# A gated MLP behind attention: the last rows' side work cut into small pieces, its operands by VectorE, and the order of the low parts

## Chip, cores and metric

One core of one Trainium2 chip. The metric is the device time of one execution in microseconds (us), as the median of a few runs. PE is TensorE's matmul stream (PEld its weight loads), DVE is VectorE, ACT is ScalarE, POOL is GpSimd, SP is SyncE, whose queue issues most DMAs.

## The reference

```python
mod = (silu(c) @ w_mod).reshape(1, 6, 1, 576)     # sa, ca, ga, sb, cb, gb
h = layernorm(x) * (1 + ca) + sa                  # x: 1 x 2048 x 576
x = x + ga * attention(h, wqkv, wo)               # 32 heads of 18
h = layernorm(x) * (1 + cb) + sb
x = x + gb * ((sigmoid(h @ w_gate) * (h @ w_up)) @ w_down)   # F = 4608
```

Everything is float32. The kernel splits each float32 operand of a product into a high part (a cast to `fp32r`) and a low part (the difference), and sums high x high, high x low and low x high.

## The kernel before

The program has two stages. The first, up to 1602 us, is projections and attention. In its last part it also makes the second layer norm of rows 0 to 1023 and writes their operands to DRAM; of rows 1024 to 2047 it has only done most of the output projection (`x1p`, and `oend` for the columns that come last). The second stage is the gated MLP, and the change lies wholly in it.

**Turns.** `seq` is a list of 252 turns: 2 halves of the rows, 18 blocks of 256 MLP columns (`NB`), 7 products each, in the order `ORDER` = 1, 6, 2, 7, 5, 4, 3; turn 6 is below the turn of product 6, and so on. Seven products replace eight, since a block of 2 x 2 products (gate and up over two groups of 128 columns, two groups of 512 rows) is formed by a scheme of Strassen's kind. One product is 14 matmuls of 128x128 by 128x512 (`product`, L1050). Their left operands `w` come from the raw weights or from sums of them (`S1`, `S2`, `S3`, made on POOL by `weights_sums`); the right operands `X` are seven operands of the rows, which stay in SBUF for a whole half.

**Weights.** In the first half of the turns the weights are made while the turns run, `LOOK` = 4 turns ahead: `weights_high` copies the high part on ACT (L1031), `weights_low` subtracts the low part on DVE (L1040, L1041) and saves the operand to DRAM over SP (`ws`, L1042). The table `LOWS` says in which turn which low part is made; the three of turn 7 stand one after the other, behind the turn's down sums. In the second half the weights come back by DMA.

**A block.** Product 1 is copied by ACT to `p1`. DVE adds products and partial sums (L1254, L1265, L1270, L1276, L1281). Products 2, 5, 4 and 3 complete one gated group each: `gate` takes the sigmoid (ACT), the product with the other half (DVE), the high part `hh` (ACT); `gate_low` the low part `hl` (DVE, L1070), in the same turn. In turns 6 and 7 of the *next* block PE makes the down sums (`down`, L1090): 8 sums per turn, 6 matmuls of 128x288 each, into a PSUM pool `pd` of 3 buffers; DVE adds each sum into `Oa` (L1094), and this frees the buffer.

**The last rows.** While the first half's turns run, the operands of rows 1024 to 2047 must be made for the second half. The generator `last_rows` does it in steps: the end of the output projection (PE, DVE), layer norm statistics and scaling (DVE, some POOL), transposes (PE) that ACT scales and SP writes to DRAM (`ln_spill`, `hs`), and at last, three times, `operand_parts`: from four 128x512 blocks the seven operands, with high parts by ACT (L729) and the differences and low parts by POOL (L731, L736, L740), written to `xs`. The main loop takes steps of it from block 0's turn 5 on, in turns 6 and 7 of each block, and in others where a step has been marked as light by yielding `True`. In the last block of the first half, `X` is reloaded from `xs`, one operand per turn.

**Order.** From turn 7 on (`ORDERED`) the order of PE, DVE and ACT is that of the program's text; POOL and SP follow a scheduler. Each engine works in order: an instruction that waits holds all behind it.

Of the kernel before, what the change touches and what calls it, by code (L numbers as in the profile page):

```python
# [15 lines left out]
F32 = mybir.dt.float32  # L16
# [27 lines left out]
LOOK = 4  # L44
LOWS = ((2,), (2,), (2,), (2, 3, 4), (), (3,), ())
NB = F // 256
# [6 lines left out]
ORDERED = 7  # L53
ROWS_FROM = 4
SECOND = 7 * NB
# [3 lines left out]
def tile_block(ctx, tc, x_in, wqkv, wo, w_gate, w_up, w_down, c_in, w_mod, out):  # L59
# [646 lines left out]
    def ln_spill(zs, ch, psum, pool, put):  # L706


        for g in range(2):
            for i in range(3):  # L710
                pt = psum()
                for j, z in enumerate(zs):
                    nc.tensor.transpose(pt[:, j * P : (j + 1) * P], z[:, g, i * P : (i + 1) * P], ident)
                ev = pool.tile([P, 512], F32, name="ev", bufs=2)
# [339 lines left out]

    def gate(st, t, f, r):

        if t is None:
            t = ep.tile([P, 512], F32, name="sg")
            nc.scalar.activation(t, st["a"][0], AF.Sigmoid)  # L1059
            nc.vector.tensor_mul(t, st["a"][1], t)  # L1060
        else:
            nc.scalar.activation(t[:, 0:512], t[:, 0:512], AF.Sigmoid)  # L1062
            nc.vector.tensor_mul(t[:, 0:512], t[:, 0:512], t[:, 512:1024])  # L1063
            t = t[:, 0:512]
        nc.scalar.copy(st["hh", r][:, f, :], t)  # L1065
        return st, t, f, r
# [9 lines left out]

    def down(st, r):

        wh, wl = st["wd"]
        hh, hl = st["hh", r], st["hl", r]  # L1080
        for j in range(4):
            t = 4 * r + j
            rows = slice(j * P, (j + 1) * P)
            for h in range(2):
                cols = slice(h * HALF, (h + 1) * HALF)
                acc = pd.tile([P, 512], F32, name="d")
                n = 0
                for f in range(2):
                    for a, w in ((hh, wh), (hh, wl), (hl, wh)):
                        nc.tensor.matmul(  # L1090
                            acc[:, :HALF], a[:, f, rows], w[:, f, cols], start=n == 0, stop=n == 5
                        )
                        n += 1
                nc.vector.tensor_add(Oa[:, t, cols], Oa[:, t, cols], acc[:, :HALF])  # L1094
# [35 lines left out]
    pd = ctx.enter_context(tc.tile_pool(name="pd", bufs=3, space=PSUM))  # L1130

    def last_rows():


        def psum():
            return pd.tile([P, 512], F32, name="d")

        with tc.tile_pool(name="fin", bufs=1, side="right") as pool:
            w = pool.tile([P, 2, 2, D], F32R, name="w")
            nc.gpsimd.dma_start(w, wod)  # L1140
            for t0 in (0, 4):
                od = pool.tile([P, 4, 256], F32, name="od")
                nc.sync.dma_start(od[:, :, 0:192], oend[:, t0 : t0 + 4, :])
                nc.sync.dma_start(od[:, :, 192:256], oend[:, t0 : t0 + 4, 128:192])
                yield True
                yield
                pt = psum()
# [5 lines left out]
                nc.vector.tensor_sub(ol, pt, oh.bitcast(F32))  # L1153
                yield
                pt = psum()
# [4 lines left out]
                nc.vector.tensor_copy(om[0:64], pt[0:64])  # L1160
                nc.vector.tensor_copy(omh[64:P], pt[64:P])
                nc.vector.tensor_sub(om[64:P], pt[64:P], omh[64:P].bitcast(F32))
                xts = []
                for j in range(-1, 4):
                    if j < 3:
                        xts.append(pool.tile([P, D], F32, name="xt", bufs=2))
                        nc.sync.dma_start(xts[-1], x1p[:, t0 + j + 1, :])
                    if j < 0:
                        yield 0
                        continue  # L1170
                    rows = slice(j * P, (j + 1) * P)
                    xt = xts[j]
                    for h in range(2):
                        cols = slice(h * HALF, (h + 1) * HALF)
                        acc = psum()
                        ts_ = ((oh, 0, 0), (oh, 1, 0), (ol, 0, 0), (om, 0, 1), (om, 1, 1))
                        for n, (a, i, k) in enumerate(ts_):
                            nc.tensor.matmul(
                                acc[:, :HALF], a[:, rows], w[:, i, k, cols], start=n == 0, stop=n == 4
                            )  # L1180
                        nc.vector.tensor_add(xt[:, cols], xt[:, cols], acc[:, :HALF])
                    nc.sync.dma_start(x1d[:, t0 + j, :], xt)
                    yield

# [3 lines left out]
        with tc.tile_pool(name="zp2", bufs=1, side="right") as zp:  # L1188
            for ch in (2, 3):
                zs = []  # L1190
                for t in range(4 * ch, 4 * ch + 4):
# [3 lines left out]
                    zs.append(z)  # L1195
                yield True
                yield
                for j, z in enumerate(zs):
                    ln_stats(zp, z[:, :, 0:HALF], mv2[:, 4 * ch + j, :])
                    if j % 2:  # L1200
                        yield
                four = slice(4 * ch, 4 * ch + 4)
                yield from ln_scales_steps(zp, mv2[:, four, :], rs2[:, four])
                for j, z in enumerate(zs):
                    ln_rows(z, 4 * ch + j, z[:, :, 0:HALF], nc.vector)
                    if j % 2:
                        yield True if j > 1 else None
                yield True
                yield from ln_spill(zs, ch, psum, zp, modulated)
        with tc.tile_pool(name="xop2", bufs=2) as pool:  # L1210
# [7 lines left out]
            for i in range(3):  # L1218
                blocks = get()
                for (g, r), t in zip(((0, 0), (0, 1), (1, 0), (1, 1)), blocks):  # L1220
                    cols = slice(HW + r * 512, HW + (r + 1) * 512)
                    nc.sync.dma_start(t, hs[g, i, :, cols])
                yield True
                yield True
                for _ in operand_parts(1, i, blocks, parts, nc.scalar.copy, nc.gpsimd, nc.sync):
                    yield True

# [6 lines left out]
    rows2 = last_rows()  # L1234
    light = True
    before = None
    for n, (hf, b, k) in enumerate(seq):
        if n == ORDERED:
            manual.enter_context(tc.manual_schedule(engines={mybir.EngineType.PE, mybir.EngineType.DVE, mybir.EngineType.Activation}))
        st, kept = block(n), None  # L1240
        if SECOND <= n + LOOK < len(seq):
            weights_high(block(n + LOOK), seq[n + LOOK][2])
        if k == 1:
# [3 lines left out]
            for v in range(2):  # L1247
                nc.scalar.copy(half(st["p1"], v), st["a"][v])
        elif k == 6:
            st["b_"] = banks()  # L1250
# [4 lines left out]
        elif k == 2:  # L1255
            product(st, 2, st["a"], False)
            for r in range(2):
                st["hh", r] = ep.tile([P, 2, 512], F32R, name=f"hh{r}")
                st["hl", r] = ep.tile([P, 2, 512], F32R, name=f"hl{r}")
            kept = gate(st, None, 0, 0)  # L1260
        elif k == 7:
# [4 lines left out]
        elif k == 5:  # L1266
            st["c"] = banks()
            product(st, 5, st["c"], True)
            for v in range(2):
                nc.vector.tensor_add(half(st["u3"], v), st["c"][v], half(st["u3"], v))  # L1270
            kept = gate(st, st["u3"], 1, 1)
            down_weights(st)
        elif k == 4:
            product(st, 4, st["b_"], False)
            for v in range(2):
                nc.vector.tensor_add(half(st["p1"], v), st["b_"][v], half(st["p1"], v))  # L1276
            kept = gate(st, st["p1"], 1, 0)
        else:
            product(st, 3, st["c"], False)
            for v in range(2):  # L1280
                nc.vector.tensor_add(half(st["u2"], v), st["c"][v], half(st["u2"], v))  # L1281
            kept = gate(st, st["u2"], 0, 1)
        if before is not None and k in (6, 7):
            down(before, k - 6)
        if n + LOOK < SECOND:
            weights_high(block(n + LOOK), seq[n + LOOK][2])
        at = n % 7
        lows = list(LOWS[at])
        if lows:
            weights_low(n + lows.pop(0))  # L1290
        if kept:
            gate_low(*kept)
        if n >= ROWS_FROM and (at in (1, 3) or light):
            light = next(rows2, None)
        while lows:
            weights_low(n + lows.pop(0))
        if n >= ROWS_FROM and (at == 1 and light is None or at in (1, 3) and light is True):
            light = next(rows2, None)
# [5 lines left out]
        if hf == 0 and b == NB - 1:  # L1304
            s = ORDER.index(k)
            nc.gpsimd.dma_start(X[s], xs[1, s])
    for r in range(2):
        down(before, r)
    manual.close()
# [27 lines left out]
```

## Time and profile before

| | |
|---|---|
| median of 3 runs | 2940.77 us (2938.65 to 2940.89) |
| the profiled execution | 2941.94 us, of it span 2940.2 us |
| PE, DVE, ACT, POOL busy | 2851.2, 2205.7, 1564.5, 707.2 us |
| first half's turns | 1602.20 to 2286.93 us, 684.73 us, PE busy 651.19, DVE busy 532.27 |
| one block of the second half | 34.96 us, PE busy 34.96 |

Rows of the profile name line, engine, operation, `out<-in` and shape; "idle before" is the time in which the engine waited ahead of the instruction, with what ended the wait. The windows view gives the busy time of each engine in a stretch, the TensorE clock that was granted (PEclk, 1.00 is full) and the DMA engines' share.

### The profile page before, as it was taken

How to read it: one execution, taken by the hardware profiler on the slowest of the kernel's cores; microseconds unless marked ns; L12 is line 12 of the kernel's file. 1: busy time of each engine (PE TensorE's matmuls, PEld its weight loads, DVE VectorE, ACT ScalarE, POOL GpSimd, SP SyncE). 2: the span in 40 equal slices, each digit the busy share in tenths (PEclk: the TensorE clock that was granted, in tenths of full speed). 3: DMA queues.
4: the chain of work that ended last, by engine and by line, in shares of the span. 5: the costliest groups of instructions: out<-in, count | busy, mean ns of one | idle time of the engine just before them, and what ended most of it. 6: DMA issues, size and time to landing. Idle time of an engine off the chain costs nothing. (4 is left out here: it accounts for less than half of the span.)

```text
span 2940.2 us, 46375 instructions
## 1 busy us (share of the span) xinstructions
PE 2851.2 (97%) x17141; PEld 1884.8 (64%) x17141; DVE 2205.7 (75%) x4015; ACT 1564.5 (53%) x2941; POOL 707.2 (24%) x869
## 2 busy tenths in 40 slices
PE   7999999999999999999999999999989999999998
PEld 5964333343444443444444888888778888888887
DVE  7277888888899988999982777878777555555555
ACT  2216889999987778998788333233332111111111
POOL 3022015444212111761103222222562100000000
PEclk9999999999999999999999999999999999999999
DMA  5344124333222110322135756565767854454443
GB/s 164 125 152 140 48 79 139 133 121 123 83 56 76 35 56 23 103 95 66 55 100 184 250 209 238 195 229 207 276 225 252 320 172 167 168 168 165 158 166 119
DMA packets 136386, 429.26 MB, mean 146 GB/s; under 512 B 19100, under 2 KB 55968, under 8 KB 123872
## 3 DMA queue, kind: packets, MB, share of 16 engines
q1 hardware_dynamic: 119664, 344.20, 34.6%
q0 software_dynamic: 16496, 82.10, 8.0%
q8 instruction: 135, 2.21, 0.3%
q14 instruction: 91, 0.75, 0.1%
HBM read 267.77 MB, written 157.95 MB: 145 GB/s over the span
## 5 line engine op out<-in xcount | busy, mean ns | idle before, releaser
L455 DVE TENSOR_REDUCE mx<-s 128x1 f32<-128x512 f32 x1696 | 1076.1, 683 | 124.2 <-PE s L449 108.0
L931 ACT ACTIVATE p<-s 128x512 f32<-128x512 f32 x2048 | 1069.1, 612 | 148.7 <-PE s L449 78.2
L449 PE MATMUL s<-k,q 54*128 54x512 f32 x1920 | 608.1, 451 | 12.8 <-ACT p L931 5.7
L551 PE MATMUL o<-p,vaug 128*32 128x512 f32 x4096 | 554.9, 607 | 0.4 <-ACT p L931 0.4
L927 PE MATMUL s<-q,k 56*128 56x512 f32 x1920 | 551.9, 425 | 0.9 <-issue 0.2
L1090 PE MATMUL d<-wd,hh 128*128 128x288 f32 x2304 | 467.7, 298 | 24.2 <-DVE Oa L1094 19.5
L927 PEld LDWEIGHTS s<-q,k 56*128 56x128 f32 x1920 | 260.4, 186 | 295.1 <-DVE mx L455 185.5
L449 PEld LDWEIGHTS s<-k,q 54*128 54x128 f32 x1920 | 273.6, 184 | 250.0 <-ACT p L931 170.9
L1090 PEld LDWEIGHTS d<-wd,hh 128*128 128x128 f32 x2304 | 377.5, 190 | 34.1 <-DVE Oa L1094 23.4
L1094 DVE TENSOR_TENSOR Oa<-Oa,d 128x288 f32<-128x288 f32 x576 | 257.7, 453 | 173.7 <-PE d L1090 169.7
L1050 PE MATMUL x<-k,w 128*128 128x512 f32 x1512 | 357.9, 391 | 2.4 <-ACT w L1031 2.4
L1090 PE MATMUL d<-wd,hl 128*128 128x288 f32 x1152 | 342.6, 297 | 0.0
L1050 PEld LDWEIGHTS x<-k,w 128*128 128x128 f32 x1512 | 282.6, 189 | 59.8 <-ACT w L1031 2.6
L1062 ACT ACTIVATE u<-u 128x512 f32<-128x512 f32 x72 | 45.5, 632 | 424.6 <-DVE u L1270 384.9
L1050 PE MATMUL x<-big,w 128*128 128x512 f32 x1008 | 238.8, 392 | 10.6 <-DVE u L1270 10.6
L1050 PE MATMUL x<-w,w 128*128 128x512 f32 x1008 | 235.2, 390 | 1.1 <-DMA w<-ws 1.1
L1050 PEld LDWEIGHTS x<-big,w 128*128 128x128 f32 x1008 | 189.2, 189 | 53.0 <-issue 12.5
L1090 PEld LDWEIGHTS d<-wd,hl 128*128 128x128 f32 x1152 | 218.7, 190 | 0.0
L1050 PEld LDWEIGHTS x<-w,w 128*128 128x128 f32 x1008 | 187.3, 188 | 38.5 <-issue 1.3
L551 PEld LDWEIGHTS o<-p,vaug 128*32 128x32 f32 x4096 | 83.4, 108 | 163.9 <-issue 152.2
L1059 ACT ACTIVATE sg<-x 128x512 f32<-128x512 f32 x36 | 21.5, 598 | 311.8 <-PE x L1050 311.7
L1096 POOL DMA_DIRECT2D out_dram<-Oa x16 | 8.7, 542 | 606.7 <-DVE Oa L1094 606.7
(215 smaller groups left out, 2996.9 us busy)
## 6 DMA issues: line engine op xcount, KB each, us to landing
ws<-w SPq DMA_DIRECT2D x126, 640.0 KB
w<-ws SPq DMA_DIRECT2D x126, 640.0 KB
wd<-wds SPq DMA_DIRECT2D x36, 1152.0 KB
k<-kd SPq DMA_DIRECT2D x60, 360.0 KB
wds<-w POOLq DMA_DIRECT2D x18, 1152.0 KB, 4.5
k<-kd SPq DMA_DIRECT2D x60, 180.0 KB
w<-in_B_w_down_dram POOLq DMA_DIRECT2D x18, 576.0 KB, 4.5
q<-qd SPq DMA_DIRECT2D x64, 144.0 KB
```

What stands on the lines that cost most here:

```text
L449: nc.tensor.matmul(sp, qs[rows, qt * P : (qt + 1) * P], ks[rows, at * 512 : (at + 1) * 512], start=True, stop=True,)
L455: nc.vector.tensor_reduce(to, sp, axis=AX.X, op=ALU.max)
L551: nc.tensor.matmul(acc[32 * j : 32 * j + 32, :], vaug[:, kt, (2 * p + h) * VW : (2 * p + h) * VW + 32], probs[2 * c + h], start=kt == 0, s ...
L927: nc.tensor.matmul(sT, ks[rows, kcols], qs[rows, c * 512 : (c + 1) * 512], start=True, stop=True)
L931: state["exp"] = nc.scalar.activation(pr, sT, AF.Exp, scale=SCALE)
L1050: nc.tensor.matmul(acc[v], w[:, v, a, :], X[s][:, b, :], start=first and n == 0, stop=n == 6, skip_group_check=not first,)
L1059: nc.scalar.activation(t, st["a"][0], AF.Sigmoid)
L1062: nc.scalar.activation(t[:, 0:512], t[:, 0:512], AF.Sigmoid)
L1090: nc.tensor.matmul(acc[:, :HALF], a[:, f, rows], w[:, f, cols], start=n == 0, stop=n == 5)
L1094: nc.vector.tensor_add(Oa[:, t, cols], Oa[:, t, cols], acc[:, :HALF])
L1096: nc.gpsimd.dma_start(out_rows[:, 8 * st["half"] + t, :], Oa[:, t, 0:D])
```

## The change

1. `last_rows` yields, in place of light or not, a pair: the DVE cost in us of its next step, and how many turns that step must stay away. A table `ROOM` gives each turn's room for steps (in the order of `ORDER`); a turn takes up to 2 steps (turns 1, 6, 2, 7) or 1. Steps are cut smaller: one row group's statistics, one row scaling, one low part. The steps begin in block 0's turn 6 (`ROWS_FROM` 1), and what is left at the last block's start would be done there at once. By the table the last step lies in block 16's turn 7, and none is left.
2. `operand_pieces` takes the place of `operand_parts` for these rows: differences and low parts by DVE, high parts still by ACT, one piece per step.
3. `gate` is split: the sigmoid; `gate_high`, the multiplication and the high part; `gate_low` is put off to the next turn in turns 5, 4 and 3 of the first half (`behind`, `flush`).
4. The low parts of turn 7 are made between its down sums (after sums 4, 6 and 8), that of turn 6 after sum 4, that of turn 2 ahead of `gate_high`; the one of turn 4 moves to turn 5, ahead of `gate_high`. `weights_high` of turns 7 and 5 moves to the turn's start.
5. `ev` has 3 buffers in place of 2. At the very end, the last group's multiplication and low part go between the down sums.

```diff
-LOWS = ((2,), (2,), (2,), (2, 3, 4), (), (3,), ())
+ROOM = (1.5, 2.2, 1.0, 1.5, 0.0, 0.7, 0.0)
-ROWS_FROM = 4
+ROWS_FROM = 1
...
-    def down(st, r):
+    def down(st, r, between):
...
                 nc.vector.tensor_add(Oa[:, t, cols], Oa[:, t, cols], acc[:, :HALF])
+                if 2 * j + h in between:
+                    between[2 * j + h]()
...
+    def operand_pieces(i, blocks, parts):
+        b11, b12, b21, b22, t3 = blocks
+        ho = {}
+        def high(k, t):
+            ho[k] = parts(), t
+            nc.scalar.copy(ho[k][0][:, 0, :], t)
+        def low(k):
+            s = ORDER.index(k)
+            to, t = ho.pop(k)
+            if i < 2:
+                nc.vector.tensor_sub(to[:, 1, :], t, to[:, 0, :].bitcast(F32))
+                nc.sync.dma_start(xs[1, s, :, i : i + 4 : 3, :].bitcast(F32), to.bitcast(F32))
+            else:
+                for q in (32, 96):
+                    lo = to[q : q + 32, 0, :]
+                    nc.vector.tensor_sub(lo, t[q : q + 32], lo.bitcast(F32))
+                    if q == 32:
+                        yield 0.7, 0
+                nc.sync.dma_start(xs[1, s, :, 2, :].bitcast(F32), to[:, 0, :].bitcast(F32))
+        nc.vector.tensor_sub(t3, b22, b12)
+        high(1, b11)
+        high(3, b22)
+        yield 0.7, 1
+        yield from low(1)
+        yield 0.7, 0
...
     for n, (hf, b, k) in enumerate(seq):
...
+        early = n + LOOK >= SECOND or at in (3, 4)
+        if early and n + LOOK < len(seq):
             weights_high(block(n + LOOK), seq[n + LOOK][2])
...
         elif k == 5:
...
-            kept = gate(st, st["u3"], 1, 1)
+            kept = gate(st, st["u3"]), 1, 1
+            weights_low(n + 4)
             down_weights(st)
...
+        if kept and not final:
+            behind.append(gate_high(st, *kept))
+        if before is not None and k == 6:
+            down(before, 0, {3: lambda: weights_low(n + 2)})
+        elif before is not None and k == 7:
+            down(before, 1, {3: lambda: weights_low(n + 2), 5: lambda: weights_low(n + 3), 7: lambda: weights_low(n + 4)})
...
-        if n >= ROWS_FROM and (at in (1, 3) or light):
-            light = next(rows2, None)
+        room, count = ROOM[at], 0
+        while n >= soonest and piece <= room and count < (2 if at < 4 else 1):
+            room, count = room - piece, count + 1
+            got = next(rows2, None)
...
-    for r in range(2):
-        down(before, r)
+    down(before, 0, {
+        1: lambda: behind.append(gate_high(st, *kept)),
+        3: flush,
+    })
+    down(before, 1, {})
```

**DVE around turn 7 of block 12.** `u` is the partial sum of the group that turn 5 completes (the first row adds product 7, the row with L1270 or L1338 product 5), `Oa` the down sums, `w` low parts of weights, `hl` a gated low part, `B` and `ho` the last rows' blocks and operands. Before:

```order
L1265 TENSOR_TENSOR u_25271<-x,p_25100 128x512 x2
L1094 TENSOR_TENSOR Oa<-Oa,d 128x288 x8
L1040 TENSOR_TENSOR w<-raw_24734,w 128x2x256
L1041 TENSOR_TENSOR w<-raw_24734,w 64x2x128
L1040 TENSOR_TENSOR w<-S_24976,w 128x2x256
L1041 TENSOR_TENSOR w<-S_24976,w 64x2x128
L1040 TENSOR_TENSOR w<-raw_25016,w 128x2x256
L1041 TENSOR_TENSOR w<-raw_25016,w 64x2x128
L1270 TENSOR_TENSOR u_25271<-x,u_25271 128x512 x2
L1063 TENSOR_TENSOR u_25271<-u_25271 128x512
L1070 TENSOR_TENSOR hl_25241<-u_25271,hh_25240 128x512
L1276 TENSOR_TENSOR p_25100<-x,p_25100 128x512 x2
```

And now, from the same addition on (L1333 was L1265, L1100 was L1094, L1338 was L1270):

```order
L1333 TENSOR_TENSOR u_25316<-x,p_25161 128x512 x2
L1100 TENSOR_TENSOR Oa<-Oa,d 128x288 x4
L1040 TENSOR_TENSOR w<-raw_24816,w 128x2x256
L1041 TENSOR_TENSOR w<-raw_24816,w 64x2x128
L1100 TENSOR_TENSOR Oa<-Oa,d 128x288 x2
L1040 TENSOR_TENSOR w<-S_25051,w 128x2x256
L1041 TENSOR_TENSOR w<-S_25051,w 64x2x128
L1100 TENSOR_TENSOR Oa<-Oa,d 128x288 x2
L1040 TENSOR_TENSOR w<-raw_25085,w 128x2x256
L1041 TENSOR_TENSOR w<-raw_25085,w 64x2x128
L1153 TENSOR_TENSOR ho<-B,ho 128x512
L1338 TENSOR_TENSOR u_25316<-x,u_25316 128x512 x2
```

The three low parts have moved from behind the eight down sums to between them, and one piece of the operands (L1153) stands where POOL had it before. What follows the last row now is a weight's low part, then the multiplication, then the next group's additions, and only then `hl`.

**SP around the load of the down weights (`wd`) in block 12.** `ws` are saved weights, `xs` saved operands. Before:

```order
L1042 DMA ws<-w 128x1280 x2
L732 DMA xs<-ho 128x2x512 x3
L1222 DMA B<-hs 128x512
L1074 DMA wd<-wds 128x2304
L1042 DMA ws<-w 128x1280 x3
L732 DMA xs<-ho 128x2x512
L863 DMA raw_25399<-in_B_w_gate_dram 128x2x256
```

And now:

```order
L1042 DMA ws<-w 128x1280 x2
L1154 DMA xs<-ho 128x2x512
L1042 DMA ws<-w 128x1280 x3
L1154 DMA xs<-ho 128x2x512
L1042 DMA ws<-w 128x1280
L1080 DMA wd<-wds 128x2304
L863 DMA raw_25431<-in_B_w_gate_dram 128x2x256
```

The load of `wd` stood ahead of three saves of weights; it now stands behind them and one more, which is that of the low part made in turn 5.

**DVE at the end of the program.** `p` and `u` are the last two groups' sums. Before:

```order
L1276 TENSOR_TENSOR p_32022<-x,p_32022 128x512 x2
L1063 TENSOR_TENSOR p_32022<-p_32022 128x512
L1070 TENSOR_TENSOR hl_32127<-p_32022,hh_32126 128x512
L1281 TENSOR_TENSOR u_32043<-x,u_32043 128x512 x2
L1063 TENSOR_TENSOR u_32043<-u_32043 128x512
L1070 TENSOR_TENSOR hl_32129<-u_32043,hh_32128 128x512
L1094 TENSOR_TENSOR Oa<-Oa,d 128x288 x16
```

And now:

```order
L1345 TENSOR_TENSOR p_32022<-x,p_32022 128x512 x2
L1069 TENSOR_TENSOR p_32022<-p_32022 128x512
L1076 TENSOR_TENSOR hl_32127<-p_32022,hh_32126 128x512
L1351 TENSOR_TENSOR u_32043<-x,u_32043 128x512 x2
L1100 TENSOR_TENSOR Oa<-Oa,d 128x288 x2
L1069 TENSOR_TENSOR u_32043<-u_32043 128x512
L1100 TENSOR_TENSOR Oa<-Oa,d 128x288 x2
L1076 TENSOR_TENSOR hl_32129<-u_32043,hh_32128 128x512
L1100 TENSOR_TENSOR Oa<-Oa,d 128x288 x12
```

The multiplication of the last group (L1063, now L1069) and its low part have moved to behind the second and the fourth down sum.

More of the change, by code (lines that the diff above doesn't have):

```diff
@@ L1053, in product, with gate @@
                 )
-    def gate(st, t, f, r):
+    def gate(st, t):
         if t is None:
@@ L1222, in last_rows @@
                     nc.sync.dma_start(t, hs[g, i, :, cols])
[L1223 to L1226, printed above, removed]
+                yield 0.7, 2
+                yield from operand_pieces(i, blocks, parts)
     def banks():
@@ L1304, in tile_block @@
         if hf == 0 and b == NB - 1:
+            if n == 7 * (NB - 1):
+                for _ in rows2:
+                    pass
             s = ORDER.index(k)
             nc.gpsimd.dma_start(X[s], xs[1, s])
-    for r in range(2):
-        down(before, r)
+    down(before, 0, {
[3 more added lines that the diff above has]
+    down(before, 1, {})
     manual.close()
```

132 lines of the change are left out of this document (82 added, 50 removed).

## The prediction

> **What bounds the kernel now.** I read the page first, then the windows view by stage, then PE's waits, then the timeline around the longest of them. On the page PE is busy nearly throughout and DVE much of the time.
>
> ```profile
> span 2940.2 us, 46375 instructions
> PE   7999999999999999999999999999989999999998
> DVE  7277888888899988999982777878777555555555
> ```
>
> The dent in PE's row lies in the first half's turns. The windows view (PE, PEld, DVE, ACT, POOL busy, then granted clock and DMA share) shows that half; block 14, of the worst; blocks 16 and 17, in which no step of the last rows is left; and a block of the second half.
>
> ```profile
> 1602.20:2286.93 684.73, 651.19 (x3540) 572.26 (x3541) 532.27 (x919) 217.09 (x334) 228.80 (x195) 0.99 0.67 237
> 2129.67:2174.01 44.34, 38.46 (x196) 33.65 (x195) 34.28 (x50) 15.55 (x25) 29.82 (x23) 0.92 0.76 268
> 2216.00:2251.46 35.46, 35.22 (x195) 31.16 (x194) 27.25 (x48) 11.10 (x18) 9.45 (x8) 1.00 0.57 210
> 2251.46:2286.93 35.47, 35.24 (x195) 31.15 (x194) 26.55 (x48) 10.28 (x17) 5.70 (x8) 1.00 0.89 325
> 2847.63:2882.59 34.96, 34.96 (x196) 31.12 (x194) 19.26 (x35) 6.05 (x10) 0.00 (x0) 1.00 0.51 166
> ```
>
> A block costs PE 34.96 us, and the second half runs at exactly that: nothing can be gained there. The first half's excess is made of PE's waits (the waits view, from 1603 to 2287 us: total, times, longest), of what each costs at its restart, and of a slower clock.
>
> ```profile
> PE d L1090 <- DVE Oa L1094: 18.1, 15, 4.0
> PE x L1050 <- DVE u L1270: 10.6, 6, 3.3
> PE d L1090 <- ACT ev L1186: 4.7, 2, 2.8
> ```
>
> They come to 33.4 us in 23 waits, all behind DVE or ACT, none behind a DMA. The timeline shows the kind: in block 14's turn 7 three low parts stand between the last down sum and L1270, whose additions free the buffers that product 3 needs.
>
> ```profile
> 2160.81 1.39 DVE L1041 TENSOR_TENSOR w<-raw,w 64x256 fp32r<-64x256 f32 x1
> 2162.23 1.67 DVE L1040 TENSOR_TENSOR w<-S,w 128x512 fp32r<-128x512 f32 x1
> 2167.06 1.37 DVE L1041 TENSOR_TENSOR w<-raw,w 64x256 fp32r<-64x256 f32 x1
> 2168.46 1.29 DVE L1270 TENSOR_TENSOR u<-x,u 128x512 f32<-128x512 f32 x2
> 2207.75 0.42 DVE L1041 TENSOR_TENSOR w<-raw,w 64x256 fp32r<-64x256 f32 x1
> 2208.21 0.69 DVE L1040 TENSOR_TENSOR w<-S,w 128x512 fp32r<-128x512 f32 x1
> ```
>
> The same forms take 0.42 and 0.69 us a block later. In block 14 POOL was busy for 29.82 us against 9.45, so POOL's operand work not only takes its own time but stretches DVE's.
>
> **Slow clock.** After the longer waits the clock drops to half:
>
> ```profile
> 2100.65:2104.06 3.41, 3.41 (x17) 3.41 (x16) 1.16 (x3) 0.00 (x0) 0.00 (x0) 0.50 1.00 350
> 2141.61:2145.02 3.41, 3.41 (x16) 3.41 (x15) 1.14 (x3) 0.00 (x0) 0.00 (x0) 0.50 1.00 353
> 2168.91:2172.33 3.42, 3.03 (x7) 2.48 (x8) 2.58 (x4) 1.60 (x3) 3.03 (x3) 0.50 0.68 268
> 2185.98:2192.81 6.83, 5.70 (x24) 5.71 (x25) 3.16 (x8) 0.00 (x0) 3.05 (x3) 0.50 0.67 228
> ```
>
> PE was busy for 3.41 + 3.41 + 3.03 + 5.70 = 15.55 us of these at half speed, which costs 7.8 us. All four lie in blocks 13 to 15, where POOL makes operands. The Trainium skill, in "TensorE: Matmul & The Clock Gate" (What's actually happening), lets the clock fall only after an idle window of about 3.4 us; by that only the longest wait (4.0 us) would count and this term would be 2.9 us. The trace shows drops with shorter waits too, so the row decides.
>
> **The change part by part.** *Waits that go.* The lows of turn 7 move between the down sums, where DVE is short of work: a sum takes PE 0.80 us (successive sums start at 2222.34, 2223.13 and 2223.93), an addition 0.45. Rows of the groups view over the first half:
>
> ```profile
> L1094 DVE TENSOR_TENSOR Oa<-Oa,d 128x288 f32<-128x288 f32 x272 | 119.9, 452 | 80.7 <-PE d L1090 79.2
> L1070 DVE TENSOR_TENSOR hl<-u,hh 128x512 fp32r<-128x512 f32 x35 | 25.2, 719 | 24.4 <-ACT hh L1065 24.4
> L736 POOL TENSOR_TENSOR ho<-B,ho 32x512 fp32r<-32x512 f32 x14 | 20.6, 1475 | 2.4 <-issue 1.5
> L731 POOL TENSOR_TENSOR ho<-B,ho 128x512 fp32r<-128x512 f32 x14 | 19.6, 1406 | 9.8 <-ACT ho L729 9.8
> L740 POOL TENSOR_TENSOR B<-B 128x512 f32<-128x512 f32 x12 | 16.6, 1387 | 4.1 <-ACT w L1031 3.4
> 2222.34 0.42 PE L1090 MATMUL d<-wd,hh 128*128 128x288 f32 x2
> 2223.13 0.43 PE L1090 MATMUL d<-wd,hh 128*128 128x288 f32 x2
> 2223.93 0.42 PE L1090 MATMUL d<-wd,hh 128*128 128x288 f32 x2
> ```
>
> Eight sums leave 8 x 0.35 = 2.8 us; three lows of 0.69 + 0.42 take 3.3. So DVE ends turn 7's sums about 1 us behind PE, and even with 1.5 us of steps it reaches L1270's additions about when product 5 ends; product 3 comes 3.2 us (14 matmuls) after that. The 10.6 us should go. `hl` one turn later takes the wait for ACT's `hh` (24.4 us in the L1070 row, about 0.7 each) out of DVE's queue ahead of the additions on which the down sums of turn 6 hang. The 4.7 us behind `ev` go with the third buffer and with transposes spread over more turns.
>
> *Operands by DVE.* 40 POOL instructions (14 + 14 + 12) become 40 of DVE. Their form is that of `hl` (two SBUF inputs, 128x512), so 40 x 0.72 = 28.8 us, over blocks 10 to 16: 4.1 us a block, 5.7 in the fullest (8 pieces). On top of the 27.25 us of block 16 that makes 33 of PE's 35: it fits, closely. The bounds of one piece are 0.45 us (the L1094 row) and 1.67 (L1040 beside POOL); I take 0.72, the same form. POOL loses 56.8 us, and with it the stretch of DVE's other work.
>
> *PE.* It does the same matmuls; only their places change. Block 16's restart: 35.22 busy against 34.96, so 0.26 us lost beside a wait of 0.24.
>
> ```profile
> 2225.11 0.54 PE L1090 MATMUL d<-wd,hh 128*128 128x288 f32 x2 [0.24 <-DVE Oa L1094]
> ```
>
> 23 waits x 0.26 = 6.0 us. At stake in the first half: 33.4 + 6.0 + 7.8 = 47.2 us.
>
> *What stays.* In block 16 turn 6's additions start late:
>
> ```profile
> 2223.41 1.29 DVE L1254 TENSOR_TENSOR u<-x,p 128x512 f32<-128x512 f32 x2
> ```
>
> Product 6 had ended at 2222.34, 1.1 us before. Ahead of them three waits of 0.7 us for `hh` (turns 5, 4, 3) leave DVE's queue, so without steps it would be 1.0 us early; with 1.4 us of steps in turn 1 (at the most; 12 blocks of 17 have some) and 0.7 in turn 4 it is 1.1 late, as now. I take the loss that blocks 16 and 17 show without any steps: 0.5 us a block, 17 x 0.5 = 8.5 us. Bounds: 0 (DVE always in time), and 25 (1.5 us in each). Block 0 stays.
>
> *The end.* The last down sums wait once for DVE's chain through the last group:
>
> ```profile
> 2917.55 0.42 PE L1090 MATMUL d<-wd,hh 128*128 128x288 f32 x2
> 2921.48 0.53 PE L1090 MATMUL d<-wd,hh 128*128 128x288 f32 x2 [1.40 <-DVE Oa L1094]
> 2917.61 1.28 DVE L1281 TENSOR_TENSOR u<-x,u 128x512 f32<-128x512 f32 x2
> 2920.37 0.69 DVE L1070 TENSOR_TENSOR hl<-u,hh 128x512 fp32r<-128x512 f32 x1 [0.68 <-ACT hh L1065]
> ```
>
> Now two additions into `Oa` come right behind L1281, from 2918.9 on, and free the first buffer before PE's fourth sum (2917.55 + 3 x 0.80 = 2919.9) needs it. With its restart 1.7 us go; the next thing late would be `hl`, needed only by the ninth sum, 8 x 0.80 = 6.4 us after the first.
>
> *Sum.* 47.2 - 8.5 + 1.7 = 40.4 us. The profiled execution took 2941.94 us (span 2940.2 and 1.7 around it), 1.2 above the median of 2940.77: 2941.9 - 40.4 = 2901.5 there, **2900.5** against the median.
>
> *Queues.* SP's load of `wd` now stands behind the save of a low part that DVE makes after product 5:
>
> ```profile
> 2242.13 0.32 SPq L1074 DMA_DIRECT2D wd<-wds  x1
> 2243.08:2247.32 4.24, 4.24 (x20) 3.54 (x19) 4.07 (x7) 0.00 (x0) 2.35 (x2) 1.00 0.97 335
> 2257.81 0.42 PE L1090 MATMUL d<-wd,hh 128*128 128x288 f32 x2
> ```
>
> Its 1152 KB went by at about 335 GB/s from 2243.08 to 2247.32 (estimate: together with some other traffic), and PE used it at 2257.81. The wait moves the issue by one product, two additions and a low part, 3.2 + 1.3 + 1.1 = 5.6 us; of the 10.5 us of slack 4.9 remain, so I take it at nothing. ACT's early copies (L1031, 0.83 us) stand ahead of the sigmoid in turn 5, and the copy there waits for POOL's sum `S2`, which follows a low part now made in turn 7's sums.
>
> **Rivals.** *DVE becomes the bound (B).* For: 33 of 35 us leave little, and each of the 40 pieces can hit one of POOL's weight sums, 9.45 us of POOL a block; L1040 shows 1.67 for 0.69. If every piece pays that 1.0 us, blocks 10 to 16 need 7 x 27.25 + 28.8 + 40 = 260 us of DVE for 245 of PE: 15 us more, 2916. Against: POOL is busy a quarter of the time. The Trainium skill, "SBUF — State Buffer" (Who interferes with whom), says that a VectorE instruction with two SBUF inputs and a GpSimd one that reads SBUF block each other for a whole instruction; the rows agree, since L1094 with its one PSUM input keeps 0.45.
>
> *ACT's queue is held by `S2` (C).* If the sum is late, the copy, the sigmoid behind it, DVE's low part and multiplication all slip. At 1.5 us a block 17 x 1.5 = 25 us come back: 2926. Against:
>
> ```profile
> 2123.74 2.64 POOL L1009 TENSOR_TENSOR S<-S,raw 128x384 f32<-128x384 f32 x2 [1.07 <-DVE w L1041]
> ```
>
> `S2` takes 2.6 us, and the low part that it waits for is now made two sums (1.6 us) ahead of turn 7's end; product 5 takes 3.2 more, so 2.2 us are in hand.
>
> *`wd` comes late (D).* One mechanism, one place: turn 6's first down sum. It decides where DVE runs over 4.9 us late at the save, or the load takes that much longer; the kernel is slower once the wait is 2.9 us in each of 17 blocks (48.9 us gained otherwise). At 3 us, with a half-clock stretch (3.41 us, 1.7 lost) each: 17 x 4.7 = 80 us, 2940.8 - 48.9 + 80 = 2972. Against: the transfer takes 4.24 us, and DVE would have to be nearly a whole turn of 6.4 us behind.
>
> **How the numbers follow.** My forecast (2893 to 2911) gets 0.70, B 0.14 (2911 to 2922), C 0.09, D 0.07. A measurement tells 0.2%, 5.9 us. Faster: forecast, B and most of C, 0.91; same 0.02 (the late end of C); slower 0.07. The range goes from no loss at all (2940.8 - 48.9 = 2892) to B's end and the early half of C, 2924; what it leaves out is D and the rest of C.
>
> **What would show it.** Right: PE's waits from 1603 to 2287 us under 10 us, the L1270 wait gone, clock 1.00 from 1610 on, blocks of 35 to 36 us plus the last rows' matmuls, POOL at 9.5 us a block in blocks 12 to 15, the 1.40 us at the end gone, 34.96 in the second half. B: DVE over 34 us in blocks 10 to 16, `ho` and `B` rows well over 0.72. C: ACT idle ahead of L1031, released by POOL. D: PE waiting for a DMA at the down sums. Wrong altogether: the first half's turns over 660 us.

## The result, and the profile after

The changed kernel takes 2897.87 us (median of 4 runs, 2895.19 to 2899.41); the kernel before, on the same chip, 2940.8 (2938.65 to 2940.89). The ratio is 0.9855, 95% interval 0.9838 to 0.9872: 42.9 us faster, where 40.3 had been forecast.

The head of the page, to be set beside that of before (slices of 1/40 of the span):

```profile
span 2893.2 us, 46407 instructions
PE   7999999999999999999999999999999999999998
DVE  7287888888899988999983778888898555555555
```

The dent in PE's row is gone, and DVE's row is fuller in its place. The windows view by stage (PE, PEld, DVE, ACT, POOL busy, then granted clock and DMA share): the first half's turns; blocks 14, 15, 16 and 17 of it; a block of the second half.

```profile
1599.31:2242.93 643.62, 639.03 (x3541) 565.92 (x3541) 538.37 (x959) 216.15 (x335) 165.40 (x155) 1.00 0.71 253
2100.61:2135.57 34.96, 34.96 (x196) 31.12 (x194) 30.80 (x54) 12.15 (x19) 9.20 (x8) 1.00 0.74 261
2135.57:2171.15 35.58, 35.23 (x196) 31.16 (x194) 33.04 (x57) 12.69 (x20) 9.44 (x9) 1.00 0.64 229
2171.15:2207.97 36.82, 35.24 (x196) 31.14 (x194) 32.12 (x56) 12.17 (x19) 8.86 (x9) 1.00 0.61 221
2207.97:2242.93 34.96, 34.96 (x196) 31.12 (x194) 25.18 (x46) 10.46 (x17) 3.33 (x6) 1.00 0.96 353
2800.00:2834.96 34.96, 34.96 (x195) 31.13 (x194) 19.27 (x35) 6.05 (x11) 0.00 (x0) 1.00 0.51 166
```

Block 14 took 44.34 us before and now takes what a block of the second half takes, with PE busy in all of it. All that PE still waits for in the first half (the waits view from 1604 to 2243 us: total, times, longest):

```profile
PE d L1096 <- DVE Oa L1100: 2.8, 4, 1.6
PE x L1050 <- DVE u L1338: 0.7, 1, 0.7
PE d L713 <- DVE Oa L1100: 0.7, 2, 0.3
PE d L1096 <- DVE ol L1211: 0.2, 1, 0.2
```

L1096 was L1090, L1100 was L1094, L1338 was L1270. 33.4 us in 23 waits have become 4.4. The timeline of DVE in block 14's turn 7 shows how:

```profile
2123.42 0.68 DVE L1040 TENSOR_TENSOR w<-raw,w 128x512 fp32r<-128x512 f32 x1
2124.12 0.42 DVE L1041 TENSOR_TENSOR w<-raw,w 64x256 fp32r<-64x256 f32 x1
2124.57 0.82 DVE L1100 TENSOR_TENSOR Oa<-Oa,d 128x288 f32<-128x288 f32 x2
2125.31 0.68 DVE L1040 TENSOR_TENSOR w<-S,w 128x512 fp32r<-128x512 f32 x1
2126.01 0.42 DVE L1041 TENSOR_TENSOR w<-S,w 64x256 fp32r<-64x256 f32 x1
2126.46 0.82 DVE L1100 TENSOR_TENSOR Oa<-Oa,d 128x288 f32<-128x288 f32 x2
2127.20 0.97 DVE L1040 TENSOR_TENSOR w<-raw,w 128x512 fp32r<-128x512 f32 x1
2128.20 1.12 DVE L1041 TENSOR_TENSOR w<-raw,w 64x256 fp32r<-64x256 f32 x1
2129.35 1.40 DVE L1158 TENSOR_TENSOR ho<-B,ho 32x512 fp32r<-32x512 f32 x2
2130.78 1.29 DVE L1338 TENSOR_TENSOR u<-x,u 128x512 f32<-128x512 f32 x2
2129.22 6.51 PE L1050 MATMUL x<-big,w 128*128 128x512 f32 x28
```

The first two low parts are each followed by two additions that PE's next sums need. The third stands behind the last sum, with two pieces of the operands, so L1338 starts 1.6 us after product 5 has ended (2129.2); its two additions are done at 2132.07. Product 3, the second half of the 28 matmuls in PE's row, starts at about 2132.4 and does not wait: L1338 is in time, by 0.3 us.

The difference of the two profiled executions (2941.94 and 2895.19), stage by stage, in us:

| | before | after | difference |
|---|---|---|---|
| start of the first half | 1602.20 | 1599.31 | -2.89 |
| first half: PE not busy | 33.54 | 4.59 | -28.95 |
| first half: PE busy | 651.19 | 639.03 | -12.16 |
| second half, to the start of its last product | 627.45 | 626.11 | -1.34 |
| from there to the span's end | 25.82 | 24.16 | -1.66 |
| outside the span | 1.74 | 1.99 | +0.25 |

The first line is no work of the change: another execution of the same kernel (run 11 below) started its first half at 1602.34. The two lines of the first half, 41.1 us, are. The 1.34 us of the second half come from its first block (36.30 us before, 34.96 after): before, PE waits there once, for 1.07 us, for a load of saved weights. The prediction did not count this, and it changes from execution to execution (35.27 us in run 11).

### The profile page after: what moved, and what is told of

It reads as the page before. It is cut to its first block, busy times and chain, and to the rows that moved or that the text cites. A ratio compares the mean times of both kernels' runs of the same rounds, so it can differ in the third digit from the quotient of the medians.

```text
span 2893.2 us, 46407 instructions
## 1 busy us (share of the span) xinstructions
PE 2836.9 (98%) x17141; PEld 1879.0 (65%) x17141; DVE 2212.7 (76%) x4055; ACT 1563.3 (54%) x2941; POOL 644.6 (22%) x829
## 4 chain that ended last, share of the span: by engine, by line
PE 89%; DVE 4%; ACT 4%; DMA 2%; issue 1%; SPq 0%; POOL 0%; DVEq 0%; POOLq 0%; ACTq 0%
PE x L1050 26%; PE o L551 17%; PE d L1096 15%; PE s L449 11%; PE s L927 11%; PE s L277 4%; ACT p L931 3%; PE s L688 2%; PE s L328 2%; DVE mx L455 1%; PE s L575 1%; DMA ws<-w 1%; DVE w L1040 0%; DVE Oa L1100 0%; DMA wm<-in_w_mod_dram 0%
## 5 line engine op out<-in xcount | busy, mean ns | idle before, releaser
L1096 PE MATMUL d<-wd,hh 128*128 128x288 f32 x2304 | 460.9, 295 | 3.0 <-DVE Oa L1100 2.8
L1096 PEld LDWEIGHTS d<-wd,hh 128*128 128x128 f32 x2304 | 373.4, 188 | 9.7 <-DVE Oa L1100 3.7
L1100 DVE TENSOR_TENSOR Oa<-Oa,d 128x288 f32<-128x288 f32 x576 | 256.3, 454 | 134.2 <-PE d L1096 128.3
L1096 PE MATMUL d<-wd,hl 128*128 128x288 f32 x1152 | 340.3, 295 | 0.0
L1096 PEld LDWEIGHTS d<-wd,hl 128*128 128x128 f32 x1152 | 216.2, 188 | 0.0
```

The costliest lines, as they stand in the source:

```text
L1096: nc.tensor.matmul(acc[:, :HALF], a[:, f, rows], w[:, f, cols], start=n == 0, stop=n == 5)
```

## The experiments

Each is one execution with its profile, and "first half" is its turns' time as in the table above (before 684.73, after 643.62); the last three kernels have four runs each. The kernel before, run beside them, took 2943.11 us at experiments 1 to 4 and 2936.41 at 5 to 8.

**1. The pieces back to POOL.** Order and pacing as in the changed kernel; the 40 differences and low parts on POOL.

```diff
-                nc.vector.tensor_sub(to[:, 1, :], t, to[:, 0, :].bitcast(F32))
+                nc.gpsimd.tensor_sub(to[:, 1, :], t, to[:, 0, :].bitcast(F32))
...
```

> The changed kernel, but the differences and low parts of the last rows' operands are made by POOL again, in the same small pieces at the same places. First half: 643.6 us in the changed kernel's profile, 684.7 before. Theory 1 (VectorE has room for the pieces, and POOL's operand work stretches VectorE's): POOL gains some 57 us in blocks 10 to 16, VectorE's L1040 and L1041 there stretch from 0.69 and 0.42 to 1.4 to 1.7 us, and the first half takes 649 to 659 us, the loss in blocks 10 to 16. Rival (the pacing in small pieces does it, the engine is indifferent): 642 to 646 us.

2900.44 us, first half 648.75: 5.1 us of the 41, just under the expected stretch. Its waits in the first half, and the timeline of one of them:

```profile
PE d L1096 <- DVE Oa L1100: 6.6, 9, 1.0
```

```profile
2113.29 5.75 POOL L1158 TENSOR_TENSOR ho<-B,ho 32x512 fp32r<-32x512 f32 x4 [8.28 <-issue]
2115.45 1.03 DVE L1040 TENSOR_TENSOR w<-S,w 128x512 fp32r<-128x512 f32 x1
2116.49 1.41 DVE L1041 TENSOR_TENSOR w<-S,w 64x256 fp32r<-64x256 f32 x1
2118.44 0.53 PE L1096 MATMUL d<-wd,hh 128*128 128x288 f32 x2 [1.02 <-DVE Oa L1100]
```

While POOL works on a piece, a low part takes DVE 1.03 + 1.41 us instead of 0.68 + 0.42; it stands between two down sums, so the additions behind it are 1.3 us late, and PE waits 1.02. Blocks 10 to 14 take 1.0 to 1.3 us longer than in the changed kernel, block 15 takes 0.4 longer, and block 16 is 0.9 shorter. The Trainium skill, "SBUF — State Buffer" (Who interferes with whom), has a VectorE instruction with two SBUF inputs contend with a GpSimd one that reads SBUF: these rows agree.

**2. The low parts behind the sums again.** Of the changed kernel, only the places of the low parts in turns 6 and 7.

```diff
-            down(before, 0, {3: lambda: weights_low(n + 2)})
+            down(before, 0, {7: lambda: weights_low(n + 2)})
...
-            down(before, 1, {3: lambda: weights_low(n + 2), 5: lambda: weights_low(n + 3), 7: lambda: weights_low(n + 4)})
+            down(before, 1, {7: lambda: [weights_low(n + i) for i in (2, 3, 4)]})
```

> The changed kernel, but the weights' low parts of turns 6 and 7 stand behind the turn's eight down sums in place of between them. Theory 1: behind the last sum VectorE has 0.45 + 3 x 1.1 + up to 1.5 us of steps + 1.3 us of additions = 5.3 to 6.6 us before product 3 can start, which PE reaches 6.35 us after that sum, so waits on L1338 of 0.3 to 1.5 us return in blocks with steps in turn 7, and the first half takes 647 to 658 us in place of 643.6. Rival (the pacing does it, the place of the lows is indifferent): under 645 us.

2929.32 us, first half 671.82: 28.2 us lost, more than was expected. The waits, and the first half in the windows view:

```profile
PE d L1096 <- DVE Oa L1100: 14.9, 16, 2.3
PE x L1050 <- DVE u L1338: 8.9, 10, 2.0
```

```profile
1603.89:2275.71 671.82, 647.91 (x3541) 567.96 (x3541) 566.34 (x959) 215.46 (x335) 176.50 (x155) 0.99 0.68 241
```

The wait for L1338 comes back, as the theory said. What it missed are the 14.9 us of waits for `Oa`. Of them 5.3 lie at turn 6's sums, as what stands behind L1338 slips too, and 9.6 at turn 7's own: the low part behind turn 6's sums pushes back the work of turn 2, and so the additions L1333 ahead of turn 7's sums (in block 13 they start 2.4 us after product 7 ends, behind a low part and an `hl` that take 1.5 us each beside POOL's sums). And DVE is busy for 566.34 us with the same 959 instructions that took 538.37, since other ones of them now lie beside POOL's sums.

**3. `hl` in its own turn again.** The end of a turn of the first half:

```diff
-        if k == 2 or hf == 1:
-            flush()
+        flush()
```

> The changed kernel, but each gated low part hl is made at the end of its own turn, as before. Theory 1: VectorE again waits about 0.7 us for ScalarE's hh three times a block, turn 6's additions come some 2 us later, and the down sums of turn 6 wait 0.5 us in blocks without steps in turn 1 and 1 to 2 with them: first half 650 to 665 us in place of 643.6. Rival (the pacing does it): under 646 us.

2913.26 us, first half 654.52: 10.9 us lost, as expected. (Another 4.8 us lie in the second half's first block, where a load of `wd` came late once.)

```profile
PE d L1096 <- DVE Oa L1100: 10.7, 9, 2.2
```

**4. VectorE alone.** The kernel before, with its steps and its order, and the differences and low parts by VectorE.

```diff
-            nc.gpsimd.tensor_tensor(to, a, b, op=ALU.subtract)
+            lo_eng.tensor_tensor(to, a, b, op=ALU.subtract)
...
-                for _ in operand_parts(1, i, blocks, parts, nc.scalar.copy, nc.gpsimd, nc.sync):
+                for _ in operand_parts(1, i, blocks, parts, nc.scalar.copy, nc.vector, nc.sync):
```

> The kernel before, with one thing of the change: the differences and low parts of the last rows' operands are made by VectorE, in the old steps and order. Theory 1: POOL's stretch of VectorE goes in blocks 12 to 15 (POOL 9.5 us a block there), but 28.8 us of pieces stand in old steps behind the lows of turn 7; the first half takes 662 to 678 us in place of 684.7, and half of the waits there stay. Rival A (the engine is the whole gain in blocks 12 to 15): 655 us or less. Rival B (without the new pacing the pieces only load VectorE): 683 us or more.

2959.68 us, first half 698.60: 13.9 slower than the kernel before. Rival B was right. Blocks 13 to 15 take 46.3, 51.8 and 44.2 us:

```profile
PE d L1090 <- DVE Oa L1094: 26.0, 18, 4.7
PE x L1050 <- DVE u L1270: 10.3, 5, 4.0
PE x L1050 <- DVE u L1281: 5.5, 3, 2.4
```

**5. Order alone.** The changed kernel's order (low parts between sums, `hl` a turn later, early high parts, the new end), with the steps, the pacing and POOL's operands of before.

```diff
-        while n >= soonest and piece <= room and count < (2 if at < 4 else 1):
...
+        if n >= ROWS_FROM and (at in (1, 3) or light):
+            light = next(rows2, None)
...
```

With the old steps come their start (`ROWS_FROM` 4) and two buffers for `ev`.

> The kernel before with the new order alone: low parts of the weights between the down sums, hl one turn behind, the early copies and the new end; the last rows' steps, their pacing and POOL as their engine are the old ones. First half 643.6 us with the whole change, 684.7 before. Theory 1 as it now stands (the order of the weights' lows and of hl is the larger part, 28 and 11 us when taken back; the engine is worth 5): 650 to 665 us, what is left lying in blocks 12 to 15 and at the steps. Rival (order and pacing need each other, as the pieces by VectorE alone cost 14 us): 670 us or more.

2920.17 us, first half 668.56: 16.2 us better than before, 3.6 short of the expected stretch. Blocks 6, 7, 9 and 10 take 35.0 to 35.9 us; 13, 14 and 15, in which the operands are made, still take 42.5, 41.5 and 45.1.

```profile
PE d L1096 <- DVE Oa L1100: 13.4, 6, 3.6
```

PE's wait behind `ev` is down to 0.4 us here (4.7 before), with two buffers still: the third buffer is not what removed most of it.

**6. Pacing alone.** The changed kernel with the two diffs of 2 and 3 together, and nothing else: small steps by each turn's room, pieces by VectorE, the old places of turn 6's and turn 7's low parts and of `hl`. The early copies, the low parts of turns 2 and 5 ahead of `gate_high` and the new end stay as in the changed kernel.

> The changed kernel with the old places of the weights' lows and of hl, both at once: what is left is the pacing in small pieces and VectorE as their engine. Theory 1 (the two parts of the order add up): 643.6 + 28 + 11 = 680 to 688 us, that is nothing gained on the 684.7 of before. Rival (both feed the same wait, so they overlap): 670 to 676 us.

2953.97 us, first half 694.87: 10.1 us slower than the kernel before, 7 more than the end of the expected stretch.

```profile
PE d L1096 <- DVE Oa L1100: 32.9, 23, 3.0
PE x L1050 <- DVE u L1338: 6.8, 8, 1.2
```

So the parts need each other: order alone gives 16, pacing with VectorE's pieces alone costs 10, all together give 41. The 10 are not the pacing's own. With the order, the new steps are worth 19.8 us (experiment 5 against 1, pieces by POOL in both: 668.56 and 648.75); without it, 3.7 (experiment 4 against this one, pieces by VectorE in both: 698.60 and 694.87). The steps fill room that, for the most part, only the order makes. The new steps with POOL's pieces in the old order were not run, and neither were the early copies by themselves.

**7. One low part twice.** L1040 is done twice in the first half, which adds 7 x 0.69 = 4.8 us of DVE to each block: to block 17 only 25.18 + 4.8 = 30, well under PE's 34.96.

```diff
         nc.vector.tensor_sub(w[:, :, 3:5, :], src[:, :, 0:2, :], w[:, :, 0:2, :].bitcast(F32))
+        nc.vector.tensor_sub(w[:, :, 3:5, :], src[:, :, 0:2, :], w[:, :, 0:2, :].bitcast(F32))
```

> The changed kernel, with the larger subtraction of each weight's low part (L1040) made twice, to the same place with the same values: seven more VectorE instructions of 0.69 us in each block of the first half, 4.8 us a block. Theory 1 (VectorE is near its bound where pieces stand, 31.4 to 33.0 us of 35 in blocks 11, 13, 15): these go to some 36 to 38 us and the block with them, block 17 (25.2 us) stays at 35; first half 655 to 675 us. Rival (VectorE still has room, since its waits shrink first): 644 to 650 us.

2953.45 us, first half 699.40: 55.8 us lost, far more than was expected. Block 17 in the windows view, and the waits of the whole half:

```profile
2263.79:2301.13 37.34, 35.75 (x196) 31.20 (x194) 30.18 (x54) 11.49 (x19) 4.81 (x8) 1.00 0.87 326
```

```profile
PE d L1097 <- DVE Oa L1101: 33.4, 43, 3.1
PE x L1051 <- DVE u L1339: 6.0, 6, 3.6
```

Block 17 has no step of the last rows, and DVE is busy for 30.18 of its 37.34 us; still it lost 2.4 us. DVE's total in a block was the wrong measure. Of the block's three waits, two of 0.41 us stand where one doubled low part lies between two additions, in turn 6 and in turn 7; the third, 0.77 us, stands at turn 6's first sums, whose additions come late. An estimate from the rows says why one low part is enough: PE fills the three buffers in 3 x 0.80 = 2.4 us; two additions of 0.45 with a low part of 1.1 between them take 2.0, with one of 1.8 they take 2.7. What DVE falls behind is carried on: over the half, 26.4 of the 33.4 us lie at turn 6's sums, where only one low part stands. Room that lies in another turn is no help to a queue that works in order.

**8. `wd` one turn later.** The load of the down weights is issued in turn 4 instead of turn 5 (`ORDER` has 4 behind 5), behind four loads of raw weights.

```diff
             weights_low(n + 4)
-            down_weights(st)
+            if hf == 1:
+                down_weights(st)
         elif k == 4:
...
             flush()
+            if hf == 0:
+                down_weights(st)
```

> The changed kernel, but the load of the down weights is issued one turn later in the program, in turn 4, so that four loads of raw weights (768 KB) stand ahead of it on SP. In the changed kernel the last of its data come 1.0 to 1.5 us ahead of PE's first use in blocks 11, 13 and 17, and 3 to 7 us ahead in others. Theory 1 (rival D of the prediction is a real edge, only not reached): some 2 us of issue and up to 3 us of data ahead of it make PE wait for a DMA at turn 6's first down sum in blocks 10 to 13 and 17, 1 to 4 us each: 648 to 660 us. Rival (the transfer simply moves into the slack): 643 to 645 us.

2939.13 us, first half 682.98: 39.4 us lost, nearly all that the change had brought, where 16 had been the most that was expected. The waits, and the timeline of the longest:

```profile
PE d L1096 <- DMA wd<-wds: 30.8, 12, 5.0
```

```profile
2135.20 0.56 SPq L1080 DMA_DIRECT2D wd<-wds  x1
2145.74 0.85 PE L1096 MATMUL d<-wd,hh 128*128 128x288 f32 x2 [4.96 <-DMA wd<-wds]
```

In this block 10.5 us pass between the issue and the first sum, 4.96 of them with PE waiting. The waits let the clock drop five times as well. The rival that was priced at 80 us (`wd` comes late) is a real cliff, one turn away.

**9, 10, 11. One step in turn 1; `wd` ahead of the low part; the changed kernel again.** The longest wait that is left, 1.58 us in block 16, has two pieces ahead of it on DVE in turn 1, and the second waits for ACT:

```profile
2177.35 0.69 DVE L1158 TENSOR_TENSOR ho<-B,ho 32x512 fp32r<-32x512 f32 x1
2179.19 0.68 DVE L1158 TENSOR_TENSOR ho<-B,ho 32x512 fp32r<-32x512 f32 x1 [1.15 <-ACT ho L1147]
2179.90 1.29 DVE L1321 TENSOR_TENSOR u<-x,p 128x512 f32<-128x512 f32 x2
2181.61 0.53 PE L1096 MATMUL d<-wd,hh 128*128 128x288 f32 x2 [1.58 <-DVE Oa L1100]
```

```diff
-        while n >= soonest and piece <= room and count < (2 if at < 4 else 1):
+        while n >= soonest and piece <= room and count < (2 if at in (1, 2, 3) else 1):
```

> The changed kernel with at most one step of the last rows in turn 1 (up to two before). In its trace the longest wait of PE in the first half (1.58 us for the down sums' buffers in block 16) stands behind two steps of turn 1 there. If the room of a single turn decides, the two waits in blocks 15 and 16 go, PE's waits for Oa fall from 2.8 to about 1 us, and the first half takes 641 to 643 us instead of 643.6: 2896 to 2898 us, 0 to 0.1% below the changed kernel. Rival, the work that leaves turn 1 waits elsewhere: the steps end later, in block 17, and the first half takes 645 us or more.

The second one issues `wd` before the save of turn 5's low part:

```diff
-            weights_low(n + 4)
             down_weights(st)
+            weights_low(n + 4)
```

> The changed kernel with the load of wd ahead of the low part of turn 5 in the program, so that SP issues it before that part's save (about 1 us earlier). If the load is hidden, as the changed kernel's trace shows with 1.0 us of slack at the least, the time stays within 0.1% (2895 to 2900 us) and only the slack grows, to about 2 us. Rival: executions in which the load is late now and then cost something, and the median falls by over 2 us.

> The changed kernel once more, as the measure for the two others on the same chip: 2895 to 2900 us, first half 643 to 645 us.

| | median (4 runs) | lowest to highest | ratio to before | first half |
|---|---|---|---|---|
| one step in turn 1 | 2894.38 | 2892.44 to 2896.01 | 0.985 (0.9835 to 0.9865) | 641.60 |
| `wd` first | 2897.23 | 2896.80 to 2898.10 | 0.986 (0.9844 to 0.9877) | 643.18 |
| the changed kernel again | 2897.77 | 2896.51 to 2900.18 | 0.9863 (0.9848 to 0.9877) | 644.13 |

With one step in turn 1, block 16 takes 35.0 us (block 15 stays at 35.6, against what was expected), and the waits of the half for `Oa` in the down sums go from 2.8 to 1.2:

```profile
PE d L1096 <- DVE Oa L1100: 1.2, 3, 0.5
```

Its runs all lie below those of the changed kernel on the same chip: 3.4 us between the medians, 2.0 to 2.5 of them seen in the first half. That is 0.12%, less than the 0.2% that counts here as told from no change, so it is shown in the trace and only probable in the time. Its median lies below the 2896 to 2898 us that were expected. It is the best version that was run. `wd` ahead of the low part changes the time by nothing; the least time between its last packet (in the trace's transfer records) and PE's first sum grows from 0.8 and 1.0 us in the two executions of the changed kernel to 1.4.

## Why the prediction was right, step by step

**What was at stake** (47.2 us: waits, restarts, half clock) and where it would go: right. PE not busy fell by 28.95 us, PE busy by 12.16 (restarts and clock, 13.8 had been reckoned for all of them). With the 1.66 us at the end the change's own lines come to 42.8 us, and the medians lie 42.9 apart. (The prediction's sum ends 0.1 to 0.2 us lower than the 2900.5 that it writes.) The wait for L1270 went by the mechanism named: experiment 2 brings it back with nothing but the low parts' places. Its cover was thinner than written: L1338 was to be reached about when product 5 ends and comes 1.6 us later in block 14, where the third low part took 0.97 + 1.12 us in place of 0.69 + 0.42.

**The shares** were not foretold part by part. The low parts, to which the text gives 10.6 us of waits, cost 28.2 us of time when put back (9.6 us of it waits at turn 7's sums, which the text did not connect with them), `hl` 10.9, the engine 5.1. That the sum came out well does not show that each part was sized well.

**What stays**, 8.5 us as 0.5 a block: too much. Of 47.2 us, 41.1 went and 6.1 stayed; nine of 18 blocks run at 34.96 or 35.0, and 1.9 of the 6.1 are the one place in block 16 (36.82 against 34.96). That turn 6's additions come 1.1 us late in every block, as in block 16 of before, did not hold. This is the term that was mis-sized, by 2.4 us.

**Operands by DVE**: 33 of 35 us in the fullest block was 33.04 (block 15), 28.8 us for the pieces was 29.9 (the six groups of them over the half; the two largest are here, busy and mean ns), POOL's 56.8 was 63.4 (228.80 to 165.40).

```profile
L1158 DVE TENSOR_TENSOR ho<-B,ho 32x512 fp32r<-32x512 f32 x14 | 10.0, 712 | 1.5 <-ACT ho L1147 1.1
L1153 DVE TENSOR_TENSOR ho<-B,ho 128x512 fp32r<-128x512 f32 x14 | 9.9, 734 | 0.1
```

But the weight that the text gave to POOL was too large. POOL's operand work does stretch DVE's; moving it to DVE is worth 5.1 us once order and pacing stand (experiment 1); without them it costs 13.9 (experiment 4). What that stretch cost by itself in block 14 of before, beside the coarse steps and the old order, was not measured. The blocks suggest that the steps weigh more: with the new order and POOL's pieces, block 14 takes 41.5 us in the old steps (experiment 5) and 36.3 in the new ones (experiment 1), where POOL's work is also spread over more blocks.

**The end**: 1.7 us foretold, 1.66 measured; the 1.40 us wait is gone, and `hl` of the last group is made before the ninth sum needs it.

**Queues**: `wd` at nothing was right, its cover was not as thick as written. 4.9 us of slack were to remain. In blocks 10 to 17 of the changed kernel between 1.0 and 4.7 did, by the transfer records, for two reasons: the issue moved by 6.6 us rather than 5.6 in the block below (15.7 us from issue to use before, 9.1 now), and the load took 6.0 to 7.2 us from issue to last packet in blocks 10 to 16, not 5.2. The least, 1.0 us, is block 17's, where the load runs beside the reload of `X` and takes 14 us. And not all of it was in hand: in experiment 8, wherever PE waited for `wd`, its first sum came 0.5 to 0.6 us after the last packet.

```profile
2205.26 0.38 SPq L1080 DMA_DIRECT2D wd<-wds  x1
2214.32 0.42 PE L1096 MATMUL d<-wd,hh 128*128 128x288 f32 x2
```

**The rivals.** B (DVE the bound): not at 33.04 us, but experiment 7 shows the bound nearby and of another kind, the room of a single turn. C (ACT held by `S2`): ACT's copies do wait for POOL's sums, 133.7 us over the half, but what stands behind them is not late for it: when the sigmoid of `u` is reached, DVE's addition is what it waits for (27.0 of 27.2 us). The two rows of ACT's groups are these:

```profile
L1031 ACT CAST w<-S 128x768 fp32r<-128x768 f32 x70 | 58.5, 836 | 133.7 <-POOL S L1009 133.7
L1061 ACT ACTIVATE u<-u 128x512 f32<-128x512 f32 x36 | 22.7, 630 | 27.2 <-DVE u L1338 27.0
```

This idle time ahead of L1031 is the sign that the prediction named for C: it came, and cost PE nothing that shows.

D (`wd` late) did not happen; experiment 8 shows it, one turn away.

**The signs** that were named for the forecast came, but for two: the wait for L1338 is not wholly gone (0.7 us, in block 0), and block 16 took 36.8 us where 35 to 36 were foretold.

## What to carry to other kernels

Count an in-order engine's room turn by turn, at the places where another engine's next work hangs on it, and not by its share of a block: DVE at 88% of a block (30.80 of 34.96 us) cost nothing where its work lay in the gaps, and at 81% (30.18 of 37.34) it cost 2.4 us where it didn't. Order and pacing are one change: the same steps were worth 19.8 us with the order and 3.7 without it. A load whose issue is moved needs its slack measured again afterwards, because the time from issue to landing changes with what runs beside it.

## What was not expected of the hardware

The half-clock stretches (3.41 us, or twice that) stood beside PE waits that were mostly shorter than that. In the turns of the thirteen profiles of this case there are 29 drops; the shortest wait beside one took 1.85 us, waits of up to 2.95 passed without one, and none of the five profiles whose longest wait was 1.58 or less had any. A wait of experiment 2 in the timeline, and the windows view behind it; then a longer wait of the kernel before, with full clock around it:

```profile
2210.97 0.77 PE L1096 MATMUL d<-wd,hh 128*128 128x288 f32 x2 [2.33 <-DVE Oa L1100]
```

```profile
2211.05:2214.46 3.41, 3.41 (x15) 3.41 (x16) 1.33 (x4) 0.00 (x0) 0.00 (x0) 0.51 0.33 107
```

```profile
2085.00 1.17 PE L1050 MATMUL x<-big,w 128*128 128x512 f32 x4 [2.95 <-DVE u L1270]
```

```profile
2082.00:2090.00 8.00, 5.05 (x23) 4.18 (x23) 6.96 (x10) 3.14 (x5) 3.93 (x3) 1.00 0.96 360
```

What tells the one from the other stands in the times of the drops. Within an execution they start on a fixed grid of 3.413 us: in the kernel before at 2100.65, 2141.61, 2168.91 and 2185.98, which are 12, 8 and 5 steps apart. PE's idle time within the one grid step ahead separates the cases. Ahead of the 29 drops it was 1.85 us or more; in the other steps at full clock, from 8 us after the start of the turns, it was 1.73 or less, but for one of 1.89 (experiment 4). The wait of 2.95 us lies across a grid line (2083.58, five steps ahead of 2100.65), with 1.53 and 1.42 us on its two sides; the wait of 2.33 us lies within one step. So a wait of 2 to 3 us costs a slow stretch or none by where it falls on the grid, which no experiment tried to steer. The Trainium skill, "TensorE: Matmul & The Clock Gate" (What's actually happening), gives one idle window of about 3.4 us; by these rows a little over half of one such step was enough.
